# Block inverses by substitution on GpSimd with one merge on TensorE, and 64-row K^T and Q^T, in a gated delta-rule kernel followed by an MLP

## The chip, the cores and the metric

The kernel runs on one core of a Trainium2 chip. The metric is the device time of one execution in microseconds (us). Engines are named as in the profile: PE (TensorE matmul) and PEld (its weight loads), DVE (VectorE), ACT (ScalarE), POOL (GpSimd) and SP (SyncE, which here only issues DMAs). Every kernel was run several times on the chip beside the kernel before. A run is called slow here when it took over 1.5% longer than the fastest run of the same kernel; ratios use fast runs alone.

## The reference, cut to what matters

```python
B, H, S, D = 4, 8, 768, 48                     # 32 heads, 768 tokens
for t in range(S):                             # per head; state is 48 x 48; k is normalised
    y_t    = g_t * (q_t @ state)
    state += beta_t * outer(k_t, v_t - k_t @ state)
x   = y as [3072, 384]
out = smelu(x @ w_in) @ w_out                  # 384 -> 2048 -> 384
```

The recurrence is computed in 24 chunks of 32 tokens. Inside a chunk the 32 coupled updates are a triangular system, so each head and chunk needs the inverse of a unit triangular 32 x 32 matrix made from K K^T. From chunk to chunk a *chain step* multiplies K^T and Q^T with the state and the inverse with what comes of it. Four chunks are a *group*; behind each group its 512 columns go through the MLP: 16 hidden tiles (`hp`), then 4 output tiles (`op`).

## The kernel before

The 32 heads sit as 4 partition blocks of 32 times 8 (index `j`). K^T and Q^T come from a DVE transpose of 32 x 32 blocks, so the 48 channels are split into 32 and 16 rows, and each product with them needs two matmuls. The inverse takes four Newton steps on PE. Cuts are marked with `...`.

```python
    raw  = ...(name="raw", bufs=2)             # k, q, v, g as loaded, one tile per group
    outp = ...(name="outp", bufs=3)            # staging of output tiles, 4 per group
    psM  = ...(name="psM", bufs=2, PSUM)       # hp and op tiles share two buffers
    ...
    def load_part(s0, off, n, names):          # 64 loads per group, all issued by SP
        ...
                    nc.sync.dma_start(out=ts[nm][32 * h4:32 * h4 + 32, c, :, :], in_=a)

    def prep_pair(p):                          # ksq = k * k (POOL), norm, kq = [k scaled, q] (POOL), vt
        ...
    def gram_step(p, c):
        kt = ktp.tile([128, J, 4, 32], F16, name=f"kt{s}", tag="kt")
        nc.vector.transpose(out=kt[:]..., in_=d["kq"][:, c]...)                    # L195
        for ch, n in ((0, 32), (1, 16)):                                           # two row halves
            for j in range(J):
                for h4 in range(4):
                    nc.tensor.matmul(gp[r, j], kt[rk, j, ch, :], kt[rk, j, ch::2, :], ...)
        ...
    def newton_pair(p):                        # for two chunks
        for lv in range(4):
            ...                                # ep: 4 + 64 matmuls, evicted to e16 by ACT
            ...                                # zp: 64 matmuls, evicted to z16 by DVE or ACT
    def chain_step(s):
        # kp = K^T state   2 x 32 matmuls, rr = kp - vt (DVE)
        # up = z rr             32,        u16 (ACT)
        # sps += K u16     2 x 32,         s16 (ACT): the next step's state
        # yp = Q^T state + upper(QK^T) u16: 2 x 32 + 32, y16 (DVE), transposed into xt
        ...
    def mlp_in(gi, xt, m):                     # hp: 3 matmuls of 512 columns; ACT, DVE and (odd m) POOL make gt
        ...
    def mlp_out(gi, b):
        op = psM.tile([128, DM], FP, name=f"op{gi}_{b}", tag="m")
        ...                                    # 16 matmuls
        nc.scalar.copy(out=ot[:], in_=op[:])
        nc.sync.dma_start(out=out[r0:r0 + GS * C, :], in_=ot[:])                   # the store: SP's queue too
```

The framework decides in which order each engine runs its instructions. "The built order" below is the order found in the built program.

## Time and profile before

The median was 601.36 us (601.04 to 601.70, 4 fast runs beside the changed kernel). These are lines of the profile's page: the span; busy us, share and instructions; the granted PE clock in 40 slices of the span (tenths of full speed); packets, MB and share of the instruction queue; the chain of waits that ended last, by engine.

```profile
span 600.9 us, 30600 instructions
...
PE 364.9 (61%) x14496; PEld 213.9 (36%) x14496; DVE 222.2 (37%) x360; ACT 149.5 (25%) x253; POOL 147.7 (25%) x168
...
PEclk9999999967855555556585557885558965578899
...
q8 instruction: 113, 1.85, 1.3%
...
issue 42%; PE 24%; SPq 9%; POOL 8%; DVE 7%; ACT 5%; DMA 4%; POOLq 0%; ACTq 0%
```

No engine is near full. The chain is 42% "issue", in which PE waits for nothing that the profile shows. PE's timeline gives this wait a shape. The columns are start and length in us, engine, line, operation, tiles and sizes, count, and in brackets the idle time just before and what ended it:

```profile
160.51 0.58 PE L203 MATMUL gp_3441<-kt_3439 32*32 32x64 f16 x53 [1.93 <-issue]
...
164.24 0.35 PE L226 MATMUL ep_0_3577<-al_213,zm_191 32*32 32x32 f16 x25 [1.33 <-issue]
...
167.69 0.21 PE L234 MATMUL zp_0_3648<-zm_191,e_0_3646 32*32 32x32 f16 x4 [1.57 <-issue]
...
171.42 0.18 PE L226 MATMUL ep_1_3715<-al_215,z_0_3713 32*32 32x32 f16 x1 [1.77 <-issue]
```

The gaps come about every 3.6 us, in the middle of a row of equal matmuls, once per 256 instructions; the instruction queue moved 113 packets of 16 KB for PE's 28,992 instructions. In the trace's DMA records each of these four gaps ends 1.4 to 1.5 us after one of the 16 KB packets has landed. So where PE runs many small matmuls, it waits for its own instructions. The second thing to see is how soon the groups follow each other. The first hidden tile of groups 0 to 5 started at 104.1, 206.2, 306.8, 394.7, 484.5 and 559.7 us (from the timeline): 75 to 102 us per group.

The change replaces DVE transposes. This is one of those before, in the view of its line (duration min/median/max in ns, start, shape):

```profile
L195 DVE STREAM_TRANSPOSE kt_289<-kq_217 x1: 1246/1246/1246, 33.0 to 33.0; 128x1024 f16<-128x1024 f16 x1
```

### The profile page before, as it was taken

To read this page: it belongs to the slowest core of one execution; us is meant where nothing else is said; L and a number is where in the kernel's file an instruction comes from. 1 tells how busy PE (TensorE), PEld (TensorE's weight loads), DVE (VectorE), ACT (ScalarE), POOL (GpSimd) and SP (SyncE) were. 2 spreads that over 40 slices of the span, in tenths; PEclk is the share of its full clock that TensorE was granted. 3 is DMA by queue.
4 is the path that set the end of the run, shared out by engine and by line. 5 is a ranking of instruction groups with operands and counts; after the bars stand their busy time and mean duration, and the time that the engine had idled before them with its cause. 6 is when DMAs were issued, how large, how long until landed. Compare 5 with 4: busy or idle time off the path is not lost.

```text
span 600.9 us, 30600 instructions
## 1 busy us (share of the span) xinstructions
PE 364.9 (61%) x14496; PEld 213.9 (36%) x14496; DVE 222.2 (37%) x360; ACT 149.5 (25%) x253; POOL 147.7 (25%) x168
## 2 busy tenths in 40 slices
PE   0033544658745647646877566877476875678637
PEld 0022433214433413433443443444333533444314
DVE  0131312655102435313744224744037542254351
ACT  1001111421221222222313133313234122243331
POOL 9962000635000122100611102502014321022220
PEclk9999999967855555556585557885558965578899
DMA  1797433550100000024430024410034400000101
GB/s 21 133 177 123 72 73 70 99 98 17 34 5 4 3 0 5 3 47 77 76 76 3 5 60 87 78 55 4 4 75 84 108 4 4 17 5 15 39 1 52
DMA packets 111629, 28.81 MB, mean 48 GB/s; under 512 B 106000, under 2 KB 111120, under 8 KB 111504
## 3 DMA queue, kind: packets, MB, share of 16 engines
q1 hardware_dynamic: 108800, 23.72, 20.1%
q0 software_dynamic: 2704, 3.15, 3.3%
q8 instruction: 113, 1.85, 1.3%
q14 instruction: 12, 0.10, 0.1%
HBM read 25.26 MB, written 4.72 MB: 50 GB/s over the span
## 4 chain that ended last, share of the span: by engine, by line
issue 42%; PE 24%; SPq 9%; POOL 8%; DVE 7%; ACT 5%; DMA 4%; POOLq 0%; ACTq 0%
SPq L85 8%; DMA rg_139<-in_g_dram 2%; SPq L93 2%; PE sps L280 1%; DMA rk_136<-in_k_dram 1%; DMA rv_138<-in_v_dram 1%; PE op_3_6904 L334 1%; PE op_0_9639 L334 1%; PE op_0_12434 L334 1%; PE op_1_6864 L334 1%; PE op_2_6884 L334 1%; PE op_3_16776 L334 0%; PE op_2_16756 L334 0%; PE op_3_16536 L334 0%; PE op_2_16516 L334 0%
## 5 line engine op out<-in xcount | busy, mean ns | idle before, releaser
L316 PEld LDWEIGHTS <-win 128*128 128x128 f16 x288 | 31.6, 117 | 105.7 <-issue 95.8
L203 PE MATMUL gp_291<-kt_289 32*32 32x64 f16 (+1 forms) x64 | 1.0, 236 | 34.3 <-DVE kt_289 L195 34.3
L182 POOL TENSOR_TENSOR kq_217<-rk_4716,rs_4794 128x768 f16<-128x768 f32 x1 | 1.5, 1475 | 56.6 <-DVE rs_4794 L179 56.6
L203 PEld LDWEIGHTS <-kt_289 32*32 32x32 f16 (+1 forms) x64 | 0.9, 122 | 34.3 <-DVE kt_289 L195 34.3
L327 POOL TENSOR_TENSOR r_1_4415<-rl_1_4412 128x512 f32<-128x512 f32 x1 | 1.1, 1050 | 47.1 <-ACT rl_1_4412 L319 47.1
L221 PEld LDWEIGHTS <-i_181 32*32 32x32 f16 x192 | 5.8, 96 | 10.1 <-DVE al_209 L209 5.2
L327 POOL TENSOR_TENSOR r_11_8621<-rl_11_8618 128x512 f32<-128x512 f32 x1 | 1.0, 1038 | 33.6 <-ACT rl_11_8618 L319 33.6
L280 PEld LDWEIGHTS <-kq_221 32*32 32x32 f16 x384 | 5.8, 107 | 7.4 <-issue 7.4
L156 POOL DMA_DIRECT2D win<-in_moe_w_in_dram x16 | 8.2, 516 | 0.0
L327 POOL TENSOR_TENSOR r_5_15903<-rl_5_15900 128x512 f32<-128x512 f32 x1 | 1.0, 1039 | 27.3 <-ACT rl_5_15900 L319 27.3
L280 PEld LDWEIGHTS <-kq_217 32*32 32x32 f16 x384 | 5.9, 110 | 5.0 <-issue 5.0
L327 POOL TENSOR_TENSOR r_5_13883<-rl_5_13880 128x512 f32<-128x512 f32 x1 | 1.0, 1038 | 26.1 <-ACT rl_5_13880 L319 26.1
L327 POOL TENSOR_TENSOR r_7_11108<-rl_7_11105 128x512 f32<-128x512 f32 x1 | 1.0, 1038 | 25.8 <-ACT rl_7_11105 L319 25.8
L171 DVE TENSOR_REDUCE nsq_274<-ksq_272 128x16 f32<-128x768 f32 x1 | 1.0, 954 | 13.6 <-POOL ksq_272 L169 13.6
L182 POOL TENSOR_TENSOR kq_219<-rk_136,rs_1006 128x768 f16<-128x768 f32 x1 | 1.5, 1474 | 16.4 <-DVE rs_1006 L179 16.4
L280 PEld LDWEIGHTS <-kq_219 32*32 32x32 f16 x384 | 4.5, 104 | 2.9 <-issue 2.9
L142 DVE STREAM_TRANSPOSE bt<-braw 128x192 f32<-128x192 f32 x1 | 0.4, 379 | 13.2 <-DMA braw<-in_beta_dram 13.2
L238 DVE CAST z_2_839<-zp_2_774 128x512 f16<-128x512 f32 x1 | 0.7, 692 | 12.3 <-PE zp_2_774 L234 12.3
L327 POOL TENSOR_TENSOR r_1_15595<-rl_1_15592 128x512 f32<-128x512 f32 x1 | 1.0, 1039 | 16.8 <-ACT rl_1_15592 L319 16.8
L327 POOL TENSOR_TENSOR r_1_12800<-rl_1_12797 128x512 f32<-128x512 f32 x1 | 1.0, 1039 | 16.1 <-ACT rl_1_12797 L319 16.1
L280 PEld LDWEIGHTS <-kq_223 32*32 32x32 f16 x320 | 3.7, 101 | 2.9 <-issue 2.9
L238 DVE CAST z_2_1563<-zp_2_1498 128x512 f16<-128x512 f32 x1 | 0.7, 690 | 10.6 <-PE zp_2_1498 L234 10.6
(1828 smaller groups left out, 1186.1 us busy)
## 6 DMA issues: line engine op xcount, KB each, us to landing
wout<-in_moe_w_out_dram POOLq DMA_DIRECT2D x1, 1536.0 KB, 16.4
win<-in_moe_w_in_dram POOLq DMA_DIRECT2D x8, 128.0 KB, 4.5
rk_136<-in_k_dram SPq DMA_DIRECT2D x16, 48.0 KB
rq_137<-in_q_dram SPq DMA_DIRECT2D x16, 48.0 KB
rv_138<-in_v_dram SPq DMA_DIRECT2D x16, 48.0 KB
rg_139<-in_g_dram SPq DMA_DIRECT2D x16, 48.0 KB
rk_2111<-in_k_dram SPq DMA_DIRECT2D x16, 48.0 KB
rq_2112<-in_q_dram SPq DMA_DIRECT2D x16, 48.0 KB
```

Source lines behind the costliest of these rows:

```text
L85: nc.sync.dma_start(out=ts[nm][32 * h4:32 * h4 + 32, c, :, :], in_=a)
L93: nc.sync.dma_start(out=braw[32 * h4 + 4 * j:32 * h4 + 4 * j + 4, :, :], in_=a)
L156: nc.gpsimd.dma_start(out=win[32 * h4 + p0:32 * h4 + p0 + n, kt, :], in_=moe_w_in[r0:r0 + n, :])
L171: nc.vector.tensor_reduce(out=nsq[:], in_=ksq[:], axis=AX.X, op=ALU.add)
L182: nc.gpsimd.tensor_tensor(out=kqf[:, :, 0:D], in0=kr.rearrange("p s j d -> p (s j) d"), in1=_ap(rs, [[1, 2 * J], [0, D]]), op=ALU.mult)
L203: nc.tensor.matmul(gp[r, j], kt[rk, j, ch, :], kt[rk, j, ch::2, :], start=(ch == 0 and j == 0), stop=(ch == 1), skip_group_check=True)
L221: nc.tensor.matmul(ep[r], i16[r, :], two_i[r], start=True, stop=False, skip_group_check=True)
L238: nc.vector.tensor_copy(out=z16[:], in_=zp[:])
L280: nc.tensor.matmul(sps[r, ch, j * D:j * D + D], kq[r, j, ch, :], u16[r, j], start=(s == 0 and j == 0), stop=True, skip_group_check=True)
L316: nc.tensor.matmul(hp[:], win[:, kt_, m * 128:m * 128 + 128], xt[:, kt_].rearrange("p b t -> p (b t)"), start=(kt_ == 0), stop=(kt_ == 2))
L327: nc.gpsimd.tensor_tensor(out=r2[:], in0=rl[:], in1=rl[:], op=ALU.mult)
L334: nc.tensor.matmul(op[:], gts[gi, m][:, b * GS * C:(b + 1) * GS * C], wout[:, m, :], start=(m == 0), stop=(m == NM - 1))
```

## The change

The intent was to take instructions from PE. K^T and Q^T are made on PE with 64 rows (48 used), so each product needs one matmul instead of two. Of the inverse, only one merge stays on PE: both 16 x 16 diagonal blocks are inverted on POOL by forward substitution, with one head and chunk per partition (4 x 32 = 128). A DVE transpose brings the matrices there, two bring the result back (`l16`, `x16`). To make room, the k, q and v input tiles went from two buffers to one, and the MLP's temporary tiles (`mlpt`) from four to two. Cut to its core:

```diff
+    vtp = ...(name="vtp", bufs=4)
-    mlpt = ...(name="mlpt", bufs=4)
+    mlpt = ...(name="mlpt", bufs=2)
-            t = raw.tile([128, GS, J, D], FP, name=f"r{nm}{s0}", tag=f"raw_{nm}")
+            t = raw.tile([128, GS, J, D], FP, ..., bufs=2 if nm == "g" else 1)
     ...
     def gram_step(p, c):
-        kt = ktp.tile([128, J, 4, 32], F16, name=f"kt{s}", tag="kt")
-        nc.vector.transpose(out=kt[:]..., in_=d["kq"][:, c]...)
+        kt = ktp.tile([128, J, 2, 64], F16, name=f"kt{s}", tag="kt")
+        for half in range(2):
+            tp = psN.tile([128, 4, 2, 64], FP, name=f"tp{s}_{half}", tag="n")
+            ...   # 16 matmuls against the identity
+            nc.scalar.copy(out=kt[:, 4 * half:4 * half + 4], in_=tp[:])
     ...
-    def newton_pair(p):
-        for lv in range(4): ...
+    def lanes(gi):
+        lt = lan.tile([128, 32, 32], F16, ...)
+        nc.vector.transpose(out=lt[:]..., in_=_ap(bm, [[1, 32], [64, 32]]))                             # L234
+        nc.gpsimd.tensor_copy(out=lm[:], in_=eye[:])
+        for j in range(15):
+            nc.gpsimd.tensor_tensor(out=tv, in0=<column j of lt>, in1=<row j of lm>, op=ALU.mult)       # L241
+            nc.gpsimd.tensor_tensor(out=lv, in0=lv, in1=tv, op=ALU.subtract)                            # L244
+        nc.gpsimd.tensor_copy(out=_ap(low, [[528, 2], [32, 16], [1, 16]]), in_=lm[:])
+        l16 = lan.tile([128, GS, J, 32], F16, ...)
+        nc.vector.transpose(out=_ap(l16, [[1, 32], [32, 32]]), in_=_ap(low, [[1, 32], [32, 32]]))       # L248
+        x16 = lan.tile([128, GS, J, 32], F16, ...)
+        nc.vector.transpose(out=_ap(x16, [[1, 32], [32, 32]]), in_=_ap(low, [[32, 32], [1, 32]]))       # L250
+    def merge_pair(p):
+        ...   # ep from bm, l16; e16 (ACT); zp from e16, x16; z16 (ACT)
     ...
     def chain_step(s):   # kp, sps, yp: one matmul per head where there were two
     ...
+    # per group: prep of both pairs | 4 gram steps | lanes | 2 merges, one part ahead of each chain step
```

## The prediction

> **What bounds the kernel now.** Busy shares (page, part 1) are low: PE 61%, DVE 37%, ACT 25%, POOL 25%. The chain of waits puts 42% on "issue": PE waiting for nothing shown. The timeline of PE has such gaps, 1.4 to 3.5 us, every 128 weight-load/matmul pairs, that is every 256 instructions, and the instruction queue (page, part 3) moved 113 packets, 1.85 MB: 16 KB each, one per 256 of PE's 28,994 instructions. In the packet records they start about 3.6 us apart wherever PE runs small matmuls (15 in 54 us from 151 to 205 us). So PE is limited by fetching its own instructions: 113 x 3.6 = 407 us. The Trainium skill ("Runtime: NRT & Kernel Launch", Instruction fetch mechanics) has these blocks, but calls crossing them mostly hidden; this trace contradicts that.
>
> The second limit is the MLP: where the previous group's last output tile still holds one of two PSUM buffers, tiles alternate 2.9 and 4.1 us (7.06 us a pair at 206 to 220 us, half clock); with both, 3.5 to 4.1 us a pair.
>
> **What changes.** PE instructions fall to 15,074 (built order): 59 blocks, 212 us of fetch at 3.6 us, so 195 us less. A chain step falls from 256 to 160 pairs, from 7.2 to 4.5 us, near its latency of about 3.9 us (sum of kp, rr 0.56, up, u 0.48, sps, s 0.80). Of ten Newton evictions per pair, two remain. Added: 8 ACT evictions of 0.58 us per group of four steps, three DVE transposes of about 1.2 us, and on POOL 30 dependent small operations. POOL's own sizes (512 elements 1.04 us, 768 1.47 us) give about 1.6 ns an element plus 0.2 us: an estimate of 12 to 14 us per group, plus about 1.2 us of casts.
>
> **How much is critical.** The built order is serial: MLP tiles 0 to 9, transposes and Gram of the next group, POOL inverses, merge, four chain steps, 41 remaining output matmuls, next MLP. And in groups 1 to 4 the last output tile is evicted only inside the next chain, so all 16 MLP tiles share one PSUM buffer. My steady group: MLP to tile 9, 27 us (6.1 a pair, the clock granted more often); transposes, Gram and lane transpose 15; POOL 15 with two foreign operations among them; cast and transpose back 2; merge and chain 22; output matmuls 8: 89 us. Before, late groups took 80 us, early ones 102 to 110. So most of the fetch gain is given back as unoverlapped latency.
>
> Sum: first MLP tile at about 95 us (104 before), next at 183 (206), 278, 367 (401), 456, 545 (560), then 40 us of tail.
>
> **Prediction: 584 us, 80% range 552 to 617.** Faster by over 2%: 0.54; within 2%: 0.30; slower: 0.16.
>
> **What would show it.** Instruction queue near 59 packets; "issue" far below 42%; PE matmul busy share down to about 45%, mean clock above 0.73; POOL busy up by 70 to 80 us; PE idle before the merge, released by DVE's back transpose, that by POOL, 15 us per group; MLP pairs of about 6 us; chain steps of 4.5 to 5 us.
>
> **What would make it wrong.** POOL's short strided rows costing twice my estimate (+12 us per group: slower); the clock falling to half anyway (+8 us per group); fetch proving quicker after idle stretches, so chain steps near 3.9 us (-3 us per group); MLP tiles overlapping the inverses better than the order suggests.

## The result, and the profile after

The changed kernel took 669.67 us (median of 4 fast runs, 666.74 to 670.35) against 601.36. The ratio is 1.113, with a 95% interval of 1.110 to 1.116: 11% slower, and above the predicted range. A ratio here and below is the mean time of one kernel's fast runs over the mean of the other's fast runs of the same rounds, so it is not quite the ratio of the quoted medians.

The lines of the page that answer to those of before:

```profile
span 665.0 us, 16817 instructions
...
PE 317.9 (48%) x7536; PEld 170.3 (26%) x7536; DVE 240.9 (36%) x306; ACT 149.3 (22%) x253; POOL 223.2 (34%) x356
...
PEclk9999999896555555567565579555566755557899
...
q8 instruction: 59, 0.97, 0.6%
...
issue 27%; POOL 19%; PE 19%; DVE 13%; SPq 12%; ACT 5%; DMA 3%; POOLq 0%; ACTq 0%; DVEq 0%
```

The parts that were meant to fall did fall: 59 instruction packets as predicted, PE's share from 61% to 48%, and "issue" from 42% to 27% of the chain. In the list of PE's waits, idle time put down to issue fell from 95 to 23 us, but PE's idle time in all rose from 232 to 343 us. POOL and DVE now stand in the chain instead. The clock is between 0.5 and 0.7 in nearly all slices of the middle; its mean fell from 0.730 to 0.692.

The first hidden tiles of the groups now start at 101.4, 193.5, 302.3, 407.8, 516.4 and 623.9 us. Here is the group from 302.3 to 407.8 us, by the stages that the prediction had named (read from the timeline; the first stage runs from the start of hidden tile 0 to the start of hidden tile 9, each later one from there to the end of its last operation):

| stage | predicted us | measured us |
|---|---|---|
| MLP tiles 0 to 9 | 27 | 31.1 |
| transposes, Gram, lane transpose | 15 | 18.6 |
| POOL: substitution, to the end of its cast | 15, cast not included | 16.1 |
| transposes back (`l16`, `x16`) | 2, cast included | 9.2 |
| merge and four chain steps | 22 | 25.1 |
| remaining output matmuls | 8 | 5.4 |
| sum | 89 | 105.5 |

The list of stages is right, and in the order of the built program they follow one another, though hidden tiles 10 to 15 and some output matmuls lie inside the later stages; the largest miss is in the transposes. The view of their lines:

```profile
L248 DVE STREAM_TRANSPOSE l_4802<-low_206 x1: 4685/4685/4685, 368.2 to 368.2; 128x1024 f16<-128x1024 f16 x1
...
L250 DVE STREAM_TRANSPOSE x_4804<-low_206 x1: 4809/4809/4809, 372.5 to 372.5; 128x1024 f16<-128x1024 f16 x1
...
L234 DVE STREAM_TRANSPOSE lt_4752<-bm_195 x1: 1907/1907/1907, 350.1 to 350.1; 128x1024 f16<-128x1024 f16 x1
```

They have the size and type of the 1.2 us transpose of before, and take 4.7 and 4.8 us. How little else runs meanwhile is shown by the busy times of the stretch of the substitution (first) and of the transposes (second):

```profile
core 0: us, PE busy (x) PEld busy (x) DVE busy (x) ACT busy (x) POOL busy (x), PEclk, DMA share, GB/s
352.00:368.10 16.10, 4.31 (x9) 1.16 (x9) 3.81 (x7) 2.06 (x3) 13.84 (x33) 0.50 0.00 1
368.10:377.30 9.20, 0.69 (x64) 0.68 (x64) 9.12 (x3) 0.59 (x1) 4.01 (x6) 0.50 0.00 0
```

PE works 4.3 of 16.1 us and then 0.7 of 9.2 us. This is also where the clock is at its lowest: it was 0.58 and 0.59 in the two stages before and 0.69 and 1.00 in the two after. The Trainium skill ("TensorE: Matmul & The Clock Gate", Part 1) says that half rate is the default and that activity releases it; this trace agrees, with 0.50 granted in both stretches.

The last thing to see in this profile is the MLP. Its tiles come in pairs of about 7 us, because both tiles of a pair wait for the same PSUM buffer (PE's timeline):

```profile
308.11 1.44 PE L352 MATMUL hp_2_5861<-xt_4194,win 128*128 128x512 f16 x3 [2.68 <-DVE gt_1_5857 L364]
311.10 1.44 PE L352 MATMUL hp_3_5871<-xt_4194,win 128*128 128x512 f16 x3 [1.55 <-DVE mx_2_5868 L359]
```

In the built program all 16 hidden tiles of groups 1 to 4 have the same PSUM bank. The other still holds the previous group's fourth output tile. At the start of the MLP no staging buffer is free for it, because the first one's store has not left. SP's timeline shows why:

```profile
289.71 0.33 SPq L375 DMA_DIRECT2D out_dram<-ot_3_3918  x1
290.10 9.76 SPq L87 DMA_DIRECT2D rk_3921<-in_k_dram  x15
...
315.75 7.80 SPq L87 DMA_DIRECT2D rg_3924<-in_g_dram  x16
323.65 0.40 SPq L375 DMA_DIRECT2D out_dram<-ot_0_5503  x1
```

SP issues in order. The store of `ot_0` stands behind 63 loads, and 15 loads of the next k stand behind the store of the previous group's `ot_3`. That store in turn waits for ACT to fill `ot_3` (SP's list of waits; the next group's is shown: us in total, times, longest):

```profile
SPq L375 <- ACT ot_3_5563 L373: 69.4, 1, 69.4
```

The late store is not the whole of it. `ot_0` had left by 324 us, and ACT was idle several times after that, but it evicted the fourth output tile only at 394.5 us, because its built order puts this eviction inside the next chain. So while the program runs it is the built order that keeps the bank. That the framework chose this order because it takes the store to be late was not shown by itself. The next group's preparation on POOL (`ksq`) began at 307.3 us: its loads had been issued by 299.9 us, and it then stood in POOL's order behind an operation of hidden tile 1.

### The profile page after: what moved, and what is told of

Read it like the earlier page. It is cut to its first block, busy times and chain, and to the rows that moved or that the text cites. A ratio compares the mean times of both kernels' runs of the same rounds, so it can differ in the third digit from the quotient of the medians.

```text
span 665.0 us, 16817 instructions
## 1 busy us (share of the span) xinstructions
PE 317.9 (48%) x7536; PEld 170.3 (26%) x7536; DVE 240.9 (36%) x306; ACT 149.3 (22%) x253; POOL 223.2 (34%) x356
## 4 chain that ended last, share of the span: by engine, by line
issue 27%; POOL 19%; PE 19%; DVE 13%; SPq 12%; ACT 5%; DMA 3%; POOLq 0%; ACTq 0%; DVEq 0%
SPq L87 11%; DMA rg_145<-in_g_dram 2%; SPq L95 1%; PE sps L321 1%; POOL lm_8044 L244 1%; POOL lm_4754 L244 1%; POOL lm_6399 L244 1%; POOL lm_1604 L244 1%; POOL lm_3109 L244 1%; DMA rv_144<-in_v_dram 1%; PE op_0_9671 L370 1%; PE op_0_7131 L370 1%; PE op_0_8776 L370 1%; DVE l_4802 L248 1%; DVE l_3157 L248 1%
## 5 line engine op out<-in xcount | busy, mean ns | idle before, releaser
L352 PEld LDWEIGHTS <-win 128*128 128x128 f16 x288 | 33.4, 120 | 193.2 <-issue 183.8
L210 PEld LDWEIGHTS <-kq_211 64*64 64x64 f16 x192 | 6.1, 149 | 44.7 <-POOL kq_211 L190 36.5
L266 PE MATMUL ep_660<-l_656,bm_195 32*32 32x32 f16 x64 | 0.7, 187 | 22.1 <-DVE l_656 L248 22.1
L266 PEld LDWEIGHTS <-bm_195 32*32 32x32 f16 x256 | 2.8, 99 | 32.7 <-issue 32.7
L210 PEld LDWEIGHTS <-kq_213 64*64 64x64 f16 x192 | 6.1, 149 | 18.1 <-POOL kq_213 L190 11.9
L248 DVE STREAM_TRANSPOSE l_656<-low_204 128x1024 f16<-128x1024 f16 x1 | 4.7, 4652 | 15.3 <-POOL low_204 L246 15.3
L266 PEld LDWEIGHTS <-bm_198 32*32 32x32 f16 x256 | 2.8, 99 | 25.6 <-issue 25.6
L266 PE MATMUL ep_1828<-l_1652,bm_198 32*32 32x32 f16 x64 | 0.7, 187 | 15.3 <-DVE l_1652 L248 15.3
L266 PEld LDWEIGHTS <-bm_201 32*32 32x32 f16 x256 | 2.8, 98 | 18.2 <-issue 18.2
L210 PEld LDWEIGHTS <-kq_219 64*64 64x64 f16 x128 | 4.1, 149 | 6.9 <-POOL kq_219 L190 4.3
L210 PEld LDWEIGHTS <-kq_217 64*64 64x64 f16 x128 | 3.3, 129 | 8.8 <-POOL kq_217 L190 4.3
```

Of the source, the lines that this page charges most:

```text
L210: nc.tensor.matmul(tp[rr, jj, a], d["kq"][rr, c, j, a, :], i64[rr, :], start=(jj == 0 and a == 0), stop=True, skip_group_check=True)
L248: nc.vector.transpose(out=_ap(l16, [[1, 32], [32, 32]]), in_=_ap(low, [[1, 32], [32, 32]]))
L266: nc.tensor.matmul(ep[r, c, j], bm[r, off + c, j, 0, :], l16[r, off + c, j], start=False, stop=True, skip_group_check=True)
L352: nc.tensor.matmul(hp[:], win[:, kt_, m * 128:m * 128 + 128], xt[:, kt_].rearrange("p b t -> p (b t)"), start=(kt_ == 0), stop=(kt_ == 2))
```

## The experiments

Two theories came first. *A*: the transposes are slow because they write with a stride, and cost what they take. *K*: the stores behind the loads cost the MLP its second PSUM buffer. Later ones are named where they come up. Eighteen kernels ran; all passed the comparison with the reference. This table lists them all; "own load queue" means that the loads of v and g are issued from ACT. Medians are over all four runs and ratios over the fast ones: two runs of h1 and one each of k1 and k2 were slow, and their fast medians are 585.1, 489.6 and 490.0 us. The record calls e1 to e4, f3, h1, h2 and h4 unclear by its 2% rule; beside e1 to e4 only three of seven runs of the kernel before were fast, so their intervals are wide (e1 1.046 to 1.070, e2 1.018 to 1.038, e4 0.979 to 1.011). The rounds e, f, g, h and k ran at different times, so a difference of medians across them can be off by some us.

| run | kernel | median us (range) | ratio to before |
|---|---|---|---|
| e1 | changed, contiguous transposes | 635.3 (632.3 to 639.2) | 1.058 |
| e2 | changed, stores on ACT | 618.0 (614.8 to 619.4) | 1.028 |
| e3 | changed, e1 + e2 | 593.0 (585.2 to 593.4) | 0.984 |
| e4 | before, stores on ACT | 596.3 (594.3 to 602.5) | 0.995 |
| f1 | before, 64-row K^T and Q^T alone | 601.1 (599.8 to 601.5) | 1.003 |
| f2 | before, POOL inverse alone | 659.9 (655.1 to 662.1) | 1.100 |
| f3 | changed, substitution cut to one column | 590.9 (589.7 to 591.2) | 0.986 |
| f4 | changed, e3 + own load queue | 499.1 (497.4 to 502.4) | 0.834 |
| g1 | f1, stores on ACT | 590.4 (587.8 to 591.8) | 0.973 |
| g2 | before, stores on ACT, own load queue | 546.7 (543.5 to 549.5) | 0.902 |
| g3 | f1, stores on ACT, own load queue | 483.6 (480.9 to 484.9) | 0.798 |
| g4 | changed, own load queue | 530.1 (526.1 to 531.3) | 0.874 |
| h1 | before, stores on POOL | 589.8 (583.2 to 596.9) | 0.974 |
| h2 | f1, stores on POOL | 590.9 (587.0 to 592.9) | 0.983 |
| h3 | before, single k, q, v input tiles | 602.1 (600.3 to 603.1) | 1.001 |
| h4 | changed, e1, stores on POOL | 610.8 (607.6 to 611.9) | 1.016 |
| k1 | f1, stores on ACT, every load split over SP and ACT | 490.0 (483.5 to 492.0) | 0.810 |
| k2 | f1, own load queue, stores on SP | 490.8 (484.5 to 494.9) | 0.813 |

### e1 to e4: the transposes and the stores

e1 swaps the free dimensions of the results, so that the transposes write contiguously and the merge matmuls read columns 64 bytes apart:

```diff
-        l16 = lan.tile([128, GS, J, 32], F16, ...)
-        nc.vector.transpose(out=_ap(l16, [[1, 32], [32, 32]]), in_=_ap(low, [[1, 32], [32, 32]]))
+        l16 = lan.tile([128, 32, GS * J], F16, ...)
+        nc.vector.transpose(out=_ap(l16, [[1, 1024]]), in_=_ap(low, [[1, 32], [32, 32]]))
         # x16 likewise; the merge reads l16[r, :, (off + c) * J + j]
```

> The changed kernel with the two back transposes (l16, x16) writing their output in one contiguous run; the merge's matmuls read columns 64 bytes apart instead. Theory A (the scattered output makes these two take 4.65 and 4.8 us where 1.2 was predicted, and both stand on the chain of waits): they fall to about 1.9 and 1.2 us, about 6 us less per group, 36 us in all: 634 us. Rival B (the wait is the POOL's; the merge's strided reads give it back): durations fall, time stays within 1% of 669.7. Rival C (the strided input is what is slow): l16 stays above 3 us.

Measured: 635.3 us, as theory A said. The lines of the two transposes, six of each:

```profile
L248 DVE STREAM_TRANSPOSE l<-low x6: 1892/1902/1909, 70.0 to 556.0; 128x1024 f16<-128x1024 f16 x6
...
L250 DVE STREAM_TRANSPOSE x<-low x6: 1194/1202/1216, 71.8 to 557.8; 128x1024 f16<-128x1024 f16 x6
```

The same elements with the same reads go from 4.7 to 1.9 us (`l16`) and from 4.8 to 1.2 us (`x16`) when only the writes are made contiguous. Reading with a 64-byte stride costs 1.9 against 1.2 us; writing so costs 4.7. The price on the other side is small: the merge matmuls, now with strided columns, went from 188 to 228 ns each. This confirms theory A: the ratio falls by 0.055, and 0.055 of 601 us is 33 us.

e2 and e4 move the output stores to ACT's queue, in the changed kernel and as a control in the kernel before; e3 joins e1 and e2.

```diff
-        nc.sync.dma_start(out=out[r0:r0 + GS * C, :], in_=ot[:])
+        nc.scalar.dma_start(out=out[r0:r0 + GS * C, :], in_=ot[:])
```

> The changed kernel with the output stores issued from ACT's queue instead of SP's. Theory K (stores wait on SP's queue behind 64 input loads, so the three staging tiles stay full, so the group's fourth output tile keeps its PSUM bank and the next group's 16 MLP tiles share one bank): the built order has MLP tiles alternating over both banks in all groups, so pairs should take 3.5 to 4.1 us instead of 7.1 in groups 1 to 4, tiles 0 to 9 about 19 us instead of 31: 40 to 50 us less, about 625 us. Rival (POOL's preparation of the next group paces the MLP stretch, not the bank): less than 13 us gained.

> Both edits. If the two causes are separate stretches of one serial chain, the savings add: about 36 + 45 us, 588 us. If one hides behind the other, the time stays near the better of the two single edits.

> Control: the kernel before with the stores moved to ACT's queue. Its MLP tiles also shared one bank for 5 to 12 of 16 tiles in groups 1 to 4. If instruction fetch (113 blocks of about 3.6 us = 407 us) bounds it and the MLP runs inside that, it gains little: 585 to 601 us. If the bank bounds it as much as it does the changed kernel, 40 us or more: 560 us or less.

Measured: 618.0, 593.0 and 596.3 us; all three as expected. In e2 the hidden tiles alternate between both PSUM banks in every group of the built program, MLP tiles 0 to 9 take 16.8 us instead of 31.1, and PE's timeline shows pairs at 3.5 to 4.1 us:

```profile
199.19 2.72 PE L352 MATMUL hp<-xt,win 128*128 128x512 f16 x6 [1.02 <-DVE gt L364]
203.25 1.46 PE L352 MATMUL hp<-xt,win 128*128 128x512 f16 x6 [1.34 <-DVE gt L364]
206.74 1.46 PE L352 MATMUL hp<-xt,win 128*128 128x512 f16 x6 [2.03 <-DVE gt L364]
```

So theory K holds, with the reservation made above: the edit moved the stores and with them the built order. The `mlpt` buffers are no rival here. With four of them and both PSUM banks the last group of the kernel before has pairs at 3.5 us, on one bank it has pairs at 7.1 us (213.2 to 220.3), as with two. The two costs nearly add: the ratio falls from 1.113 to 0.984 in e3, 77 us of 601, and by 33 us in e1 and 51 us in e2 alone. The kernel before gained almost nothing from the same edit, so it is the changed kernel that pays for the one PSUM buffer; that it does so because it has no other work to put under its MLP is likely, but was not tested.

### f1 to f4: the parts of the change, the substitution, the loads

f1 and f2 make one half of the change each. f3 cuts the substitution loop, with wrong values on purpose (the comparison still passed, so passing does not prove that an inverse is right; it is no valid version). f4 adds one edit to e3:

```diff
 f3:
-        for j in range(15):
+        for j in range(14, 15):
 f4:
-                    nc.sync.dma_start(out=ts[nm][...], in_=a)
+                    (nc.scalar if nm in ("v", "g") else nc.sync).dma_start(out=ts[nm][...], in_=a)
```

> The kernel before with the 64-row K^T and Q^T alone (Newton inverse kept). PE has 24,576 instructions, 96 blocks of 256, against 113. Theory F (the kernel before is bound by fetching PE instructions, one block every 3.6 us): 17 blocks x 3.6 us = 61 us less, so about 540 us (range 525 to 560), and the instruction queue shows 96 packets about 3.6 us apart. Rival (PE's idle time is latency of the chain, not fetch): the shorter chain step is partly eaten by the four added evictions per pair, and the time stays within 2% of before, 590 to 612 us.

> The changed kernel with the old 32-row K^T and Q^T, that is the GpSimd inverse alone. 19,488 PE instructions, 76 blocks. If the inverse with its serial order is the whole loss and the 64-row part a gain, this is slower than the changed kernel: a chain step is 256 pairs, at least 7.2 us instead of about 5, +2 us x 24 = about 50 us, less 4 us per group for the tp evictions that are gone: 690 to 710 us. Rival: the 64-row part (its tp evictions on ACT) is the loss; then this is faster than the changed kernel, below 650 us.

> The changed kernel with the substitution loop cut to its last column, so 28 of 30 GpSimd operations per group are gone (wrong values on purpose). Theory S (the substitution is wholly on the chain, nothing runs under it): 28 operations took about 12.6 us per group, 6 groups, 75 us less: 585 to 605 us. Rival H (it is hidden under MLP work, and the loss lies elsewhere): less than 20 us gained, above 645 us.

> The changed kernel with contiguous transposes and output stores on ACT's queue (593 us on this kernel's last run), and the loads of v and g also issued from ACT's queue, so that they no longer stand in line before the next group's k on SP's. The built order then runs MLP tiles between the chain and the GpSimd lanes. Theory Q (what is left of the serial order comes from one in-order load queue with single input buffers): the 14 us of substitution and part of the merge and chain go under MLP tiles; 20 us less in each of 5 groups, about 490 us (range 460 to 530). Rival (the dependences alone make it serial, Gram to lanes to merge to chain): 580 to 600 us, as without it.

**f1** took 601.1 us. The expectation from the fetch theory (540 us) fell: 17 blocks fewer gained nothing. PE's list of waits shows what took their place (line waited, releaser, us in total, times, longest):

```profile
PE hp L329 <- DVE gt L341: 57.3, 33, 2.7
...
PE zp L248 <- issue: 29.9, 22, 3.7
...
PE hp L329 <- DVE mx L336: 25.9, 24, 1.6
```

Summed over that list, PE's waits for "issue" fell from 95 us in the kernel before to 54 us, but its hidden tiles' waits for DVE rose from 58 to 83 us (57.3 + 25.9), and new waits of 41 us for POOL's `kq` took the place of 36 us for DVE's `kt`. PE's idle time in all fell only from 232 to 213 us, and the clock of the profiled run was 0.704 instead of 0.730. So the waits for fetch did become fewer, but other waits and a lower clock took up what they gave; which of these stands behind the fetch was not isolated.

**f2** took 659.9 us, between the two expectations. So nearly all of the loss is the inverse's, and the 64-row part on top of it gained nothing, which agrees with f1. The stages can't be compared one by one. In the same group (the one after the third hidden stage) the merge and chain took 33.4 us in f2 (375.2 to 408.6) and 25.1 us in the changed kernel (377.3 to 402.4); from the first hidden tile to the lane transpose, f2 took 34.4 us (316.4 to 350.8) and the changed kernel 49.7 (302.3 to 352.0). But the built order of f2 has 9 hidden tiles before the end of the lane transpose and 4 inside the chain, that of the changed kernel 13 and none. So what the shorter chain step is worth by itself, and what making K^T on PE and ACT costs, was not separated.

**f3** took 590.9 us, 79 us less than the changed kernel's median. The 28 operations removed took about 12.6 us per group, 75 us in six groups. So the substitution stood wholly in the chain, as the prediction had said; its cost was also sized rightly (30 operations, about 13.3 us a group; 12 to 14 predicted).

**f4** took 499.1 us. Moving two of four loads to another queue gained 94 us on e3, in the range expected by the theory that one in-order load queue is behind the serial order. In the stretches of substitution, DMA, DVE and PE now work:

```profile
core 0: us, PE busy (x) PEld busy (x) DVE busy (x) ACT busy (x) POOL busy (x), PEclk, DMA share, GB/s
230.10:245.60 15.50, 7.29 (x140) 2.95 (x140) 4.37 (x8) 3.81 (x6) 13.13 (x32) 0.67 0.22 40
303.00:318.50 15.50, 7.62 (x140) 3.25 (x140) 4.35 (x8) 3.81 (x6) 13.16 (x33) 0.50 0.07 13
```

PE is busy for 7.3 to 7.6 us of such a stretch instead of 4.3, since the built order now puts chain steps and hidden tiles there.

### g1 to g4: the same mending for every version

f4 raised the question which part of it is the change and which the loads. g1 to g3 give the kernel before and the 64-row kernel the same edits; g4 gives the changed kernel the load queue alone. (In g2's text, the fast version is f4.)

> 64-row K^T and Q^T with the Newton inverse kept, and output stores on ACT's queue. Alone the 64-row layout gave 601 us and the stores on the kernel before 596 us. In the 64-row run PE's idle time put down to issue fell from 95 to 54 us in the list of PE's waits, but waits of MLP tiles for their PSUM buffer rose from 58 to 83 us. Theory T (two limits that hide each other: fewer fetches only help when MLP tiles have both PSUM buffers): together they give the 41 us of issue and some 20 us of MLP waits, so 540 to 565 us. Rival (neither matters; the chain's dependences set the time): 590 to 602 us.

> The kernel before with stores and the loads of v and g on ACT's queue, nothing else: the same mending that took the changed kernel from 593 to 499 us (there with contiguous transposes). Theory T and the fetch limit: PE still runs 28,994 instructions in 113 blocks, so little is gained over 596 us: 580 to 600 us. Rival (the queues alone make vg_act fast, and the inverse does not matter): below 530 us.

> The kernel before with the 64-row layout, and stores and v and g loads on ACT's queue: all of the fast version but the GpSimd inverse. It separates what the inverse is worth once the queues are mended. 96 blocks against 59 of the fast version, 37 x 1.5 to 2.5 us of idle each = 55 to 90 us: 555 to 590 us if fetch counts (theory F in its weaker form), so the inverse is worth 55 us or more. Rival (the inverse brings nothing): within 2% of 499 us.

> The changed kernel with only the loads of v and g on ACT's queue; stores stay behind k and q loads on SP's, transposes stay strided. The built order has both PSUM buffers in every group and MLP tiles among the substitution. Theory Q (one in-order queue behind single input buffers makes the steady group serial): the strided transposes still cost about 6 us per group and may be partly hidden, so 500 to 550 us. Rival (the three mendings only add up: 10% from contiguity, stores and loads about a third each of the 170 us between 667 and 499): about 575 us.

Measured: 590.4, 546.7, 483.6 and 530.1 us. g1 is the rival's value, so moving the stores, which was to give the MLP both PSUM buffers, did not bring out the 64-row gain. g2 fell between its two expectations, g3 below both, and g4 within the one of the queue theory. Read together, they give the value of each part once the loads have two queues:

- The load queue is worth about 50 us to the kernel before (e4 to g2) and about 140 us to the changed kernel (669.7 to 530.1; both are medians of different rounds).
- The 64-row layout is worth 63 us (g2 to g3), where it had been worth nothing. Not all of this is fetch: PE's idle time put down to issue fell by 35 us, from 91 to 56.
- The POOL inverse is worth nothing. f4 has all that g3 has and the inverse besides, in its contiguous form, with the buffers and the build order that belong to it, and takes 15 us more (medians of different rounds). PE's idle time for issue is only 10 us there, and this brings nothing.

g3 is the best version found, 20% below the kernel before. Lines of its page:

```profile
span 483.2 us, 26149 instructions
...
PE 328.3 (68%) x12288; PEld 193.9 (40%) x12288; DVE 191.8 (40%) x336; ACT 173.7 (36%) x301; POOL 149.7 (31%) x170
...
PEclk9999999999776787997699996899997989889699
```

PE is busier than in any run so far, and the granted clock was 0.905 in the mean against 0.730 before.

### h1 to h4, k1 and k2: why a second load queue gains so much

In g1, with stores on ACT and all loads on SP, POOL waited long for k, the first step of the next group's preparation (POOL's timeline):

```profile
271.39 2.89 POOL L173 TENSOR_TENSOR ksq<-rk 128x768 f32<-128x768 f32 x2 [37.25 <-DMA rk<-in_k_dram]
```

The records of the DMAs show that loads and stores share eight completion semaphores, and in e4 the loads on SP waited 237 us in all for output stores issued by ACT. Theory L was that these semaphores hold the loads back. h1 and h2 put the stores on POOL's queue, which uses others. h3 tests the change's cut to single input tiles alone; h4 is e1 with stores on POOL.

```diff
 h1, h2, h4:
-        nc.sync.dma_start(out=out[r0:r0 + GS * C, :], in_=ot[:])
+        nc.gpsimd.dma_start(out=out[r0:r0 + GS * C, :], in_=ot[:])
 h3:
+            t = raw.tile([128, GS, J, D], FP, ..., bufs=2 if nm == "g" else 1)
```

> The kernel before with output stores on GpSimd's queue, all loads still on SP's in the old order. Theory L (loads are held back by the shared completion semaphores of the stores): the loads' 237 us of waits for stores vanish, next-group preparation runs early, and the time is near that of the run with v and g on ACT's queue, 540 to 560 us. Rival R (two load queues are what matters, for issue time or because k no longer stands behind v and g; or the built order does): as with stores on ACT's queue, 588 to 602 us.

> 64-row layout with Newton inverse, output stores on GpSimd's queue, loads all on SP's. Theory L: as the run with v and g on ACT's queue, 480 to 510 us. Rival R: as with stores on ACT's queue, 582 to 596 us.

> The kernel before with the k, q and v input tiles cut from two buffers to one, as the change does; nothing else. Theory B (single input tiles hold the next group's preparation back and are part of the change's loss): 620 to 650 us. Rival (the loads are already late because of the stores, so a buffer less changes nothing): 596 to 612 us.

> The changed kernel with contiguous transposes and output stores on GpSimd's queue, loads all on SP's. With stores on ACT's queue it was 593 us, with v and g loads there as well 499 us. The built order keeps the substitution apart from MLP tiles. Theory L: loads are free, but the built order decides, so only part is gained: 560 to 590 us. If the whole 94 us came from loads held by stores, 490 to 515 us. Rival R: 588 to 600 us.

Measured: 589.8, 590.9, 602.1 and 610.8 us. h3 says that the single input tiles cost the kernel before nothing. h2 gave the rival's value, h1 nearly so (585.1 us in its two fast runs, 588 expected), and h4 lay above every expectation, so theory L got no support, but these three are not a clean test. In h2 the loads of this k tile had been issued by 138 us, and `ksq` then stood behind stores in POOL's own order (POOL's timeline):

```profile
288.06 0.54 POOL L352 DMA_DIRECT2D out_dram<-ot  x1 [21.30 <-ACT ot L350]
288.62 2.90 POOL L173 TENSOR_TENSOR ksq<-rk 128x768 f32<-128x768 f32 x2
```

The store waits 21 us for its output tile, and the preparation waits behind it. On SP the loads were behind the stores, on ACT the loads waited for the stores' semaphores, on POOL the work itself is behind them: three places, and each time something of the next group is tied to the previous group's output. Only in g1 do the loads show as the wait: in f1, with stores on SP, `ksq` waited only 0.7 us for k, and what came before it was POOL's own built order.

k1 and k2 ask what it is about the second queue:

```diff
 k1 (64-row, stores on ACT):
+                    (nc.sync if h4 < 2 else nc.scalar).dma_start(out=ts[nm][...], in_=a)
 k2 (64-row, stores on SP):
+                    (nc.scalar if nm in ("v", "g") else nc.sync).dma_start(out=ts[nm][...], in_=a)
```

> 64-row layout with Newton inverse, stores on ACT's queue; the loads of partitions 0 to 63 on SP's queue, those of 64 to 127 on ACT's, each in the old line k, q, v, g. Theory two-queues (sharing the loads is what counts): about as with v and g on ACT's queue, 475 to 505 us. Theory line (k and q must not stand behind v, g and stores): near the 590 us of one queue, 570 to 600 us.

> 64-row layout with Newton inverse; v and g loads on ACT's queue, stores left on SP's behind k and q. If the v and g queue is what matters: within 2% of the 484 us of the run with the stores moved too, 475 to 495 us. If the stores on SP still hold k back as in the kernel before: above 540 us.

Measured: 489.6 and 490.0 us in the fast runs. In k1 each queue still has the line k, q, v, g, and it is as fast as k2; so it is sharing the loads that counts, not which tensors stand before which. And in k2 the stores are back on SP, at a ratio of 0.813 against 0.798 for g3 in other rounds, so with two load queues the stores' place is worth 1 to 2% at most.

What a second queue changes inside is only partly shown. With one queue `ksq` of group 3 began 40 to 51 us before that group's first chain step subtracted v (the kernel before: 288.6 us against `rr` at 328.3; g1: 271.4 against 322.6), with two queues about 120 us before (g3: 149.0 against 269.5). But moving DMAs also changes the built order of POOL and PE: with one queue the chain steps of a group stand together, with two there are hidden tiles between them. How much of the 100 us is loads that land earlier on the chip, and how much is an order that the framework builds because it takes the loads to be earlier, stays open: no edit was found that changed one without the other. Plain issue time, which rival R also named, is not ruled out either: SP takes 33.5 us to issue the 63 loads of a group shown above, and the share of SP's queue in the chain that ended last was 16, 7 and 10% in f1, g1 and h2 and 2, 1 and 2% in g3, k1 and k2.

## Why the prediction was wrong

It said 584 us (552 to 617), faster with a chance of 0.54. It was 670 us. Point by point:

1. **The instruction fetch: right as a fact, wrong as a price.** The blocks fell to 59, and "issue" fell. But "113 x 3.6 = 407 us", read as a limit from which "195 us less" can be taken, failed. A spacing of 3.6 us holds the time of the 256 instructions themselves: PE's idle time for issue was 95 us before, not 407, and the change took 72 us of it, not 195. Nor did idle time saved become time saved: 17 blocks less gained 0 us with one load queue (f1); with two (g2 to g3) the layout that saves them brought 63 us, 35 of them from waits for issue; 37 blocks more (g3 to f4) brought none. The Trainium skill ("Runtime: NRT & Kernel Launch", Instruction fetch mechanics) calls the cost of a block boundary mostly hidden; the 1.3 to 1.9 us gaps shown above contradict it for this kernel. The sum that gave 584 us did not rest on this price, though, but on the stages below.
2. **The serial order: right.** The prediction said that most of the fetch gain would be given back as latency that nothing overlaps. The windows (PE busy 4.3 of 16.1 us) and f3 (79 us for 75 us of POOL work) show it.
3. **The step that failed: "cast and transpose back 2", from "three DVE transposes of about 1.2 us".** The operation's size was taken from before, and its access pattern was not compared. The stage took 9.2 us without the cast. That is 7 us per group or about 43 us in six; making the writes contiguous (e1) gained 33 us.
4. **"MLP to tile 9, 27 us (6.1 a pair, the clock granted more often)".** It took 31.1 us at 7 us a pair. The single PSUM buffer was foreseen, the clock was not: it was 0.58 in this stage, and its mean over the run, which was to be above 0.73, was 0.692. That the idle serial stages pull it down fits the windows, but no run isolates it. With both buffers the stage takes 16.8 us (e2); that edit gained 51 us in all.
5. **Smaller terms.** Transposes and Gram took 18.6 us (15 predicted), merge and chain 25.1 (22), POOL 16.1 (15), the output matmuls 5.4 (8). The sum of all is 16.5 us too short in this group. Over the run, the last group's first hidden tile came at 623.9 us instead of 545: 79 us of the miss of 86.
6. **"What would make it wrong"** listed POOL at twice its estimate, which did not happen (13.3 us for the 30 operations; 12 to 14 was said), and the half clock, which did. The Trainium skill ("GPSIMD Engine Reference", 3.1 Elementwise) gives about 2.6 cycles per element for two inputs, at 1.2 GHz 2.2 ns, and a dispatch cost on top. The trace is a little below it: the first operation, of 30 elements, took 0.25 us and those of 128 about 0.45, which is 2.0 ns an element and 0.2 us fixed; the longer operations, of 512 and 768 elements, took 1.04 and 1.47 us, which is 1.7 ns an element.

So the sign was lost mainly on two sizes, the strided transposes and the MLP at half clock on one buffer. Either mending leaves the kernel slower than before (1.058, 1.028); both together bring it to 593 us, 0.984 of before (interval 0.971 to 0.997). That this is near the 584 us predicted is partly luck, since e2 gives the MLP a second buffer that the prediction had not counted on.

## What to carry to other kernels

A cost borrowed from another instruction of the same operation and size can fail when the access pattern differs, as 1.2 us became 4.7 here with strided writes, so compare the strides on the read and on the write side before the sizes. A spacing between events is not idle time: read the idle time itself from the list of waits. Before counting what fewer instructions bring, ask what wait stands next behind the fetch, and test it by making one half of the change alone. And look at the DMA queues first when a pipelined kernel runs its stages one after another: here a second queue for the loads was worth more than the whole rewrite of the inverse.

## What the Trainium skill lacked or had wrong

- "VectorE: DVE Perf Modes", The three transpose paths, gives one duration for the block transpose and says nothing of how strides change it: 128x1024 fp16 took 1.20 us dense, 1.90 us with a 64-byte read stride, and 4.7 to 4.8 us with a 64-byte write stride. "SBUF — State Buffer" (Door 1: The DMA port swizzle, the note on cachelines) says in general that crossing 16-byte lines costs; it gives no rate and does not set writes apart from reads.
- "Runtime: NRT & Kernel Launch", Instruction fetch mechanics: the boundary of a 16 KB block is not hidden where PE runs 32-row matmuls. Gaps of 1.3 to 1.9 us came every 256 instructions, about 3.6 us apart.
- "Trainium Kernel Development and Optimization", Key Constraints, says that issuing DMAs from several engines only saves issue time. What it lacks is how much that can be worth: sharing the loads between two queues took the 64-row kernel from 590.4 to 489.6 us. How much of that is issue time and how much the changed built order is open, so this does not show the page wrong.
- No page of those looked up warns that a store waiting in an in-order queue holds the loads behind it: in three groups of the changed kernel SP's queue waited 69 to 72 us for ACT to fill `ot_3`, with 63 loads standing behind that store.
